# Group normalization on Trainium2: half of each tile's sum moved from the matmuls to two accumulating passes on VectorE

## The chip, the cores and the metric

The kernel runs on one core of a Trainium2 chip. The metric is the device time in microseconds of one execution, and quoted times are medians of several executions. A difference counts as "faster" or "slower" from 2% on.

A ratio in this document is the mean time of one kernel's fast runs over that of the other kernel's fast runs of the same rounds, so it is not quite the ratio of the medians quoted beside it.

## The reference

The input `x` is 128 x 1024 x 32 x 16 in bf16. The 1024 channels form 32 groups of 32, so a group of one sample has 16,384 elements.

```python
xr = x.reshape(B, G, C // G, H, W)                       # G = 32
mu  = xr.mean(axis=(2, 3, 4), keepdims=True)
var = ((xr - mu) ** 2).mean(axis=(2, 3, 4), keepdims=True)
xn  = (xr - mu) / jnp.sqrt(var + 1e-5)
return xn.reshape(B, C, H, W) * g[None, :, None, None] + b[None, :, None, None]
```

## The kernel before

A tile is 128 partitions (4 samples x 32 groups) of F = 16,384 bf16: one partition holds one group of one sample. There are 32 tiles of 4.19 MB. Each is loaded, normalized in place and stored, so 8.4 MB move per tile. Six tile buffers are in flight.

For each tile, TensorE multiplies 512-column slices by an identity matrix and adds them up in PSUM: slices 0 to 7 (a quarter of the tile) into `pa`, slices 8 to 31 into `pb`. VectorE then sums the 512 columns. The first quarter gives an early estimate of the mean, `q`, so that ScalarE can start on the squares. The rest gives the exact mean.

```python
def M(i):                                     # TensorE
    for name, lo, hi in (("pa", 0, MQ), ("pb", MQ, NMM)):      # 8 and 24 slices
        ps = pspool.tile([P, MMN], F32, name=name)
        for k in range(lo, hi):
            ... nc.tensor.matmul(out=ps[:], lhsT=eye[:],
                    rhs=st["xt"][:, k * MMN : (k + 1) * MMN],
                    start=(k == lo), stop=(k == hi - 1)) ...

def R1(i):                                    # VectorE: exact mean
    st["negmean"] = sum_of(st["pb"], st["q"][:], "negmean")
    ...                                       # two 128x1 corrections: off, seed
```

The main loop interleaves tile i with tile i+1. `Q` squares on ScalarE, `V` gets the scales, `A` normalizes a quarter (8 of 32 VectorE instructions of 512 elements), `S` and `L` are the store and the load, both issued by one queue (SP) in program order.

```python
for i in range(NT):
    Q(i)
    if i + 1 < NT: M(i + 1); R0(i + 1)
    V(i)
    for c in range(NQ):
        A(i, c)
        ...
        if c == NQ // 2 - 1 and i + 1 < NT: R1(i + 1)
    ... S(i, 0, NQ) ...                       # the last two tiles are stored in quarters
    j = i + AHEAD                             # AHEAD = 5
    if UPFRONT <= j < NT: L(j)                # waits until the store of tile i-1 has ended
```

## Time and profile before

| | before |
|---|---|
| time, median (range) | 638.12 us (638.1 to 638.38, 3 runs) |
| span of the profile | 636.1 us |
| DMA | 268.4 MB at a mean of 422 GB/s |
| ScalarE / VectorE / TensorE busy | 79% / 65% / 45% |

The first lines are from the page of the profile: busy time, share and instructions of each engine (DVE is VectorE, ACT ScalarE, PE TensorE); DMA busy tenths and GB/s in 40 equal slices; two queues that carry instructions (packets, MB, share); and the chain of work that ended last, by engine and by line.

```profile
...
PE 288.7 (45%) x1025; PEld 113.2 (18%) x1025; DVE 412.6 (65%) x1371; ACT 499.8 (79%) x298; POOL 0.8 (0%) x6
...
DMA  9999999999999999999999999999999999999993
GB/s 373 443 430 398 429 434 432 441 429 431 431 428 433 433 437 427 434 429 429 433 431 436 433 433 431 431 430 435 433 433 435 430 431 429 437 418 439 428 422 151
...
q8 instruction: 8, 0.13, 0.1%
q14 instruction: 15, 0.12, 0.0%
...
DMA 80%; ACT 11%; issue 2%; DVE 2%; PE 1%; SPq 1%; DVEq 0%; ACTq 0%
DMA out_dram<-xt 72%; ACT ja L228 11%; DMA xt<-in_x_dram 8%; DVE xt L305 1%; PE pa L162 1%; SPq L98 1%; DVE jv L245 0%; ACT rstd L258 0%; DVE rstd L266 0%; DVEq L372 0%; DVE bia L277 0%; DVE scl L271 0%; DVE jd L177 0%; ACTq L228 0%; SPq L3
...
```

DMA is over 90% busy in every slice but the last, at about 430 GB/s in the steady part.

The stage table (length, then busy time and count of each engine, granted clock of TensorE, DMA share, GB/s) shows the same level in the middle of the run:

```profile
...
100.00:200.00 100.00, 47.21 (x168) 18.47 (x166) 71.19 (x239) 85.79 (x51) 0.00 (x0) 0.73 1.01 433
...
400.00:500.00 100.00, 46.52 (x160) 18.07 (x160) 66.11 (x221) 78.31 (x48) 0.00 (x0) 0.71 1.00 432
...
```

The table of waits (who waited for whom: us in total, times, longest) says that the engines wait for the loads:

```profile
...
PE pa L162 <- DMA xt<-in_x_dram: 298.8, 32, 19.2
DVE jd L177 <- PE pa L162: 155.8, 25, 9.8
...
```

The issuing queue's own waits show what held its next DMA: mostly an older store that had to end before its buffer could be loaded again.

```profile
...
SPq L98 <- DMA out_dram<-xt: 474.7, 26, 19.5
SPq L318 <- DVE xt L305: 89.3, 12, 26.7
...
```

The timeline of one steady tile (start, length, instruction, and in brackets the idle time before it) shows VectorE's slack.

```profile
...
510.64 0.69 DVE L177 TENSOR_SCALAR_CACHE_REDUCE jd<-pa 128x512 bf16<-128x512 f32 x1 [5.87 <-PE pa L162]
...
512.60 5.25 DVE L305 TENSOR_SCALAR xt<-xt,scl,bia 128x512 bf16<-128x512 bf16 x16
...
517.78 0.73 DVE L177 TENSOR_SCALAR_CACHE_REDUCE jd<-pb,q 128x512 bf16<-128x512 f32 x1
...
518.88 5.25 DVE L305 TENSOR_SCALAR xt<-xt,scl,bia 128x512 bf16<-128x512 bf16 x16
...
530.98 0.69 DVE L177 TENSOR_SCALAR_CACHE_REDUCE jd<-pa 128x512 bf16<-128x512 f32 x1 [6.85 <-PE pa L162]
...
537.05 0.34 SPq L98 DMA_DIRECT2D xt<-in_x_dram  x1
537.43 0.50 SPq L318 DMA_DIRECT2D out_dram<-xt  x1
...
```

Tile 27's first sum starts at 510.64 and tile 28's at 530.98, after 6.85 us of waiting. Between them stands the normalization of tile 26 (2 x 5.25 us), which ends near 524, but its store is issued only at 537.43, right after the load that waited for an older store. So VectorE has 5.5 to 6.9 us to spare in each steady tile, and this finished tile waits 13 us for the queue.

### The profile page before, as it was taken

The page shows a single profiled execution, that of the slowest core. Times are in us where ns is not written, and L with a number is a line of the kernel's source. Part 1 is how long each engine was busy: PE and PEld are TensorE (multiplying, and loading weights), DVE is VectorE, ACT ScalarE, POOL GpSimd, SP SyncE. Part 2 cuts the span into 40 slices and gives each one's busy share as a digit, 9 for nine tenths or more (in the row PEclk, how much of TensorE's full clock was granted, in tenths as well). Part 3 has the DMA queues.
Part 4 walks back from the last instruction along what each step waited for, and adds up shares of the span by engine and source line. Part 5 has one row for each costly group of instructions (what it writes and reads, how often), then busy time and mean ns, then how long its engine had stood idle before and what let it go on. Part 6 is the DMA issues. An engine that isn't in the chain of part 4 may idle for free.

```text
span 636.1 us, 3995 instructions
## 1 busy us (share of the span) xinstructions
PE 288.7 (45%) x1025; PEld 113.2 (18%) x1025; DVE 412.6 (65%) x1371; ACT 499.8 (79%) x298; POOL 0.8 (0%) x6
## 2 busy tenths in 40 slices
PE   5567604563335642356433555425553445546000
PEld 2223201221112210122111222112221112212000
DVE  1388888886686665875567756677555785668740
ACT  4899999997886777977679767797767986779920
POOL 0000000000000000000000000000000000000000
PEclk9789758766788666887567875678765787668655
DMA  9999999999999999999999999999999999999993
GB/s 373 443 430 398 429 434 432 441 429 431 431 428 433 433 437 427 434 429 429 433 431 436 433 433 431 431 430 435 433 433 435 430 431 429 437 418 439 428 422 151
DMA packets 11063, 268.70 MB, mean 422 GB/s; under 512 B 1312, under 2 KB 1312, under 8 KB 1312
## 3 DMA queue, kind: packets, MB, share of 16 engines
q1 hardware_dynamic: 10944, 268.44, 98.3%
q8 instruction: 8, 0.13, 0.1%
q14 instruction: 15, 0.12, 0.0%
q10 hardware_dynamic: 96, 0.00, 0.0%
HBM read 134.22 MB, written 134.22 MB: 422 GB/s over the span
## 4 chain that ended last, share of the span: by engine, by line
DMA 80%; ACT 11%; issue 2%; DVE 2%; PE 1%; SPq 1%; DVEq 0%; ACTq 0%
DMA out_dram<-xt 72%; ACT ja L228 11%; DMA xt<-in_x_dram 8%; DVE xt L305 1%; PE pa L162 1%; SPq L98 1%; DVE jv L245 0%; ACT rstd L258 0%; DVE rstd L266 0%; DVEq L372 0%; DVE bia L277 0%; DVE scl L271 0%; DVE jd L177 0%; ACTq L228 0%; SPq L318 0%
## 5 line engine op out<-in xcount | busy, mean ns | idle before, releaser
L228 ACT ACTIVATE ja<-xt,q 128x4096 bf16<-128x4096 bf16 x128 | 474.2, 3704 | 9.9 <-DVE jd L177 6.8
L305 DVE TENSOR_SCALAR xt<-xt,scl,bia 128x512 bf16<-128x512 bf16 x1016 | 333.5, 405 | 1.2
L162 PE MATMUL pa<-xt,eye 128*128 128x512 bf16 x256 | 109.8, 607 | 298.8 <-DMA xt<-in_x_dram 298.8
L162 PEld LDWEIGHTS <-eye 128*128 128x128 bf16 x1024 | 113.1, 113 | 474.4 <-DMA xt<-in_x_dram 300.2
L162 PE MATMUL pb<-xt,eye 128*128 128x512 bf16 x768 | 184.9, 400 | 1.0 <-DMA xt<-in_x_dram 1.0
L177 DVE TENSOR_SCALAR_CACHE_REDUCE jd<-pa 128x512 bf16<-128x512 f32 x32 | 22.1, 689 | 155.8 <-PE pa L162 155.8
L258 ACT ACTIVATE rstd<-var,eps_t 128x1 f32<-128x1 f32 x32 | 9.4, 294 | 96.4 <-DVE jv L245 96.4
L228 ACT ACTIVATION_READ_ACCUMULATOR ja<-xt,q 128x1 f32 x128 | 23.9, 186 | 0.0
L177 DVE TENSOR_SCALAR_CACHE_REDUCE jd<-pb,q 128x512 bf16<-128x512 f32 x32 | 23.7, 741 | 0.0
L245 DVE TENSOR_SCALAR_CACHE_REDUCE jv<-sq,seed 128x4 f32<-128x4 f32 x32 | 6.8, 214 | 18.9 <-ACT ja L228 18.9
L266 DVE RECIPROCAL rstd<-rstd 128x1 f32<-128x1 f32 x32 | 5.2, 164 | 11.6 <-ACT rstd L258 11.6
L277 DVE SCALAR_TENSOR_TENSOR bia<-scl,negmean,gb 128x32 f32<-128x32 f32 x32 | 8.0, 251 | 1.1
L271 DVE TENSOR_SCALAR scl<-gb,rstd 128x32 f32<-128x32 f32 x32 | 7.7, 242 | 1.1
L198 DVE TENSOR_SCALAR off<-negmean,q 128x1 f32<-128x1 f32 x32 | 6.8, 214 | 1.1
L298 ACT ACTIVATE xt<-xt,bia,scl 128x512 bf16<-128x512 bf16 x8 | 5.8, 800 | 0.8 <-DVE bia L277 0.8
L210 DVE SCALAR_TENSOR_TENSOR seed<-off 128x1 f32<-128x1 f32 x32 | 5.1, 159 | 1.1
L153 DVE COPY gb<-gb_p 128x64 f32<-128x64 f32 x1 | 0.2, 225 | 5.3 <-PE gb_p L145 5.3
L245 DVE DVE_READ_ACCUMULATOR jv<-sq,seed 128x1 f32 x32 | 2.6, 83 | 0.0
L177 DVE DVE_READ_ACCUMULATOR jd<-pa 128x1 f32 x32 | 2.6, 82 | 0.0
L113 ACT ACT_TABLE_LOAD x1 | 1.3, 1283 | 1.7 <-PEq L361 1.7
L177 DVE DVE_READ_ACCUMULATOR jd<-pb,q 128x1 f32 x32 | 2.5, 80 | 0.0
L111 DVE MEMSET eps_t<- 128x1 f32 x1 | 0.1, 59 | 0.9 <-PEq L361 0.9
(10 smaller groups left out, 1.7 us busy)
## 6 DMA issues: line engine op xcount, KB each, us to landing
xt<-in_x_dram SPq DMA_DIRECT2D x30, 4096.0 KB, 29.7
out_dram<-xt SPq DMA_DIRECT2D x30, 4096.0 KB, 39.1
xt<-in_x_dram SPq DMA_DIRECT2D x8, 1024.0 KB, 16.8
out_dram<-xt SPq DMA_DIRECT2D x8, 1024.0 KB, 25.3
gb_b<-in_g_dram ACTq DMA_DIRECT2D x1, 2.0 KB, 3.3
gb_b<-in_b_dram ACTq DMA_DIRECT2D x1, 2.0 KB, 5.3
```

What stands on the lines that cost most here:

```text
L98: nc.sync.dma_start(out=xt[:, c * w : (c + 1) * w], in_=x_v[i][:, c * w : (c + 1) * w]),
L162: nc.tensor.matmul(out=ps[:], lhsT=eye[:], rhs=st["xt"][:, k * MMN : (k + 1) * MMN], start=(k == lo), stop=(k == hi - 1),),
L177: nc.vector.tensor_scalar(out=jd[:], in0=ps[:], scalar1=-inv_n, scalar2=seed, op0=ALU.mult, op1=ALU.add, accum_out=total[:],),
L198: nc.vector.tensor_scalar(out=off[:], in0=st["negmean"][:], scalar1=1.0 / NQ, scalar2=st["q"][:], op0=ALU.mult, op1=ALU.subtract,),
L228: nc.scalar.activation(out=ja[:], in_=st["xt"][:, k * QF : (k + 1) * QF], func=ACT.Square, bias=st["q"][:], scale=1.0 / NQ, accum_out=sq[: ...
L245: nc.vector.tensor_scalar(out=jv[:], in0=st["sq"][:], scalar1=inv_n, scalar2=st["seed"][:], op0=ALU.mult, op1=ALU.add, accum_out=var[:],),
L258: nc.scalar.activation(out=rstd[:], in_=var[:], func=ACT.Sqrt, bias=eps_t[:], scale=float(NQ * NQ),),
L266: chain("dve", nc.vector.reciprocal(out=rstd[:], in_=rstd[:]))
L271: nc.vector.tensor_scalar(out=scl[:], in0=gam, scalar1=rstd[:], scalar2=None, op0=ALU.mult),
L277: nc.vector.scalar_tensor_tensor(out=bia[:], in0=scl[:], scalar=st["negmean"][:], in1=bet, op0=ALU.mult, op1=ALU.add,),
L298: nc.scalar.activation(out=span, in_=span, func=ACT.Identity, bias=bia, scale=scl),
L305: nc.vector.tensor_scalar(out=span, in0=span, scalar1=scl, scalar2=bia, op0=ALU.mult, op1=ALU.add,),
```

## The change

The intent is to relieve TensorE. The matmuls add only slices 0 to 15. The other half of the tile is added on VectorE in two `scalar_tensor_tensor` passes, each of which reads 2048 elements of quarter 2 and 2048 of quarter 3, adds them pairwise and accumulates. A small instruction combines the parts.

```diff
-        for name, lo, hi in (("pa", 0, MQ), ("pb", MQ, NMM)):
+        for name, lo, hi in (("pa", 0, MQ), ("pb", MQ, 2 * MQ)):
 ...
     def R1(i):
         st = state[i]
-        st["negmean"] = sum_of(st["pb"], st["q"][:], "negmean")
+        part = spool.tile([P, 4], F32, name="part")
+        js = jpool.tile([P, HF], BF16, name="js")          # HF = 2048
+        for h in range(2):
+            lo = 2 * QF + h * HF
+            chain("dve", nc.vector.scalar_tensor_tensor(
+                    out=js[:],
+                    in0=st["xt"][:, lo : lo + HF], scalar=1.0,
+                    in1=st["xt"][:, lo + QF : lo + QF + HF],
+                    op0=ALU.mult, op1=ALU.add,
+                    accum_out=part[:, h : h + 1]))
+        half = sum_of(st["pb"], st["q"][:], "half")
+        negmean = spool.tile([P, 1], F32, name="negmean")
+        chain("dve", nc.vector.tensor_scalar(
+                out=part[:, 2:4], in0=part[:, 0:2],
+                scalar1=-inv_n, scalar2=half[:],
+                op0=ALU.mult, op1=ALU.add, accum_out=negmean[:]))
+        st["negmean"] = negmean
```

(Line breaks tightened; the scratch tile of the sums is renamed and widened as well.)

More of the change, by code (lines that the diff above doesn't have):

```diff
@@ L56 @@
     QF = F // NQ
+    HF = QF // 2
     KQ = KC // NQ
@@ L173, in sum_of @@
         total = spool.tile([P, 1], F32, name=name)
-        jd = jpool.tile([P, MMN], BF16, name="jd")
+        jd = jpool.tile([P, HF], BF16, name="js")
         chain(
@@ L177, in sum_of @@
             nc.vector.tensor_scalar(
-                out=jd[:],
+                out=jd[:, 0:MMN],
                 in0=ps[:],
@@ L193, in R1 @@
         st = state[i]
-        st["negmean"] = sum_of(st["pb"], st["q"][:], "negmean")
+        part = spool.tile([P, 4], F32, name="part")
+        js = jpool.tile([P, HF], BF16, name="js")
+        for h in range(2):
+            lo = 2 * QF + h * HF
+            chain(
+                "dve",
+                nc.vector.scalar_tensor_tensor(
+                    out=js[:],
+                    in0=st["xt"][:, lo : lo + HF],
+                    scalar=1.0,
+                    in1=st["xt"][:, lo + QF : lo + QF + HF],
+                    op0=ALU.mult,
+                    op1=ALU.add,
+                    accum_out=part[:, h : h + 1],
+                ),
+            )
+        half = sum_of(st["pb"], st["q"][:], "half")
+        negmean = spool.tile([P, 1], F32, name="negmean")
+        chain(
+            "dve",
+            nc.vector.tensor_scalar(
+                out=part[:, 2:4],
+                in0=part[:, 0:2],
+                scalar1=-inv_n,
+                scalar2=half[:],
+                op0=ALU.mult,
+                op1=ALU.add,
+                accum_out=negmean[:],
+            ),
+        )
+        st["negmean"] = negmean
         off = spool.tile([P, 1], F32, name="off")
```

## The prediction

> **What bounds the kernel now.** DMA. The stage table shows a DMA share of 0.99 to 1.02 at 429 to 433 GB/s from 25 to 600 us (one dip to 412); 268.4 MB at 430 GB/s is 624 of the 636 us. 72% of the chain of waits is stores, in links of about 39 us for two tiles: 19.6 us per tile. The engines wait for it: in the table of waits PE sits 299 us before a tile's first matmul for the load, VectorE 156 us for those matmuls. In the timeline VectorE idles 5.5 to 6.9 us per steady tile.
>
> **What the change does per tile.** Removed: 16 of 32 matmuls, 3.5 us of PE at the dense pitch of 0.22 us. The first 8, which gate the mean estimate, stay. This buys nothing.
>
> Added on VectorE: two scalar_tensor_tensor passes of 2048 bf16 with an accumulator, and a small combining op (0.28 us). The Trainium skill, "Vector Engine (DVE) Microarchitecture Reference", section 5.1, lists the 2x modes for copy, cast, tensor_scalar and tensor_tensor, not for this op, so I assume one column per cycle at the 0.96 GHz of "VectorE: DVE Perf Modes": 2.13 us. The trace agrees with that rate for its accumulating op: 128x512 from PSUM took 0.69 us = 0.53 + 0.16. Estimate: 2.25 us (2.2 to 2.35) per pass, 4.8 us per tile in all, 153 us over 32 tiles. VectorE goes from 413 to about 565 us (89%).
>
> **How much is on the critical path.** Almost none, but it only just fits. A VectorE loop without waits takes 13.5 us now (timeline, tile 3 to tile 4: 15.8 less 2.3 waiting); it becomes 18.3 us, under the 19.6 us of DMA. The passes sit between the halves of the previous tile's normalization, so its store is ready 4.8 us later. In the steady part a finished tile now waits about 13 us (524 to 537 us) until the DMA issuer, held by an older store, sends it; that shrinks to about 8. At the start, stepping the loop with these durations, store 0 goes from 39.9 to 44.6, store 1 from 55.8 to 63, store 2 from 75 to 81 us; queued loads and stores keep DMA busy to 94. VectorE catches up by 1.3 us per tile, so from about tile 9 it waits for loads again. At the end the last tile is normalized by about 615 us instead of 610.7, while earlier stores keep DMA busy to about 615: it just fits.
>
> **Prediction.** 638.4 us, 636.5 to 642 eight times in ten. Faster by over 2%: 1%. Within 2%: 92%. Slower by over 2%: 7%.
>
> **What would show each step.** Matmuls 1025 to 513. Passes of 2.2 to 2.35 us (at 2x near 1.2 us, time unchanged). VectorE busy 550 to 580 us, its wait for PE down from 156 to under 60 us. ScalarE's busy time unchanged. DMA flat at about 430 GB/s with no hole before 110 us. The chain still stores; finished tiles issued on the release of an older store, not of VectorE.
>
> **What would make it wrong.** A pass above about 2.6 us: the loop (13.8 us plus two passes) then nears the DMA period, and soon VectorE bounds everything; at half rate, 4.3 us each, the loop is 22.4 us and the time about 740 us. Or a hole in DMA near 75 to 95 us, or a late last store, costing a few us.

## The result, and the profile after

| | before | after |
|---|---|---|
| time, median (range), same chip | 638.11 us (638.02 to 638.38, 4 runs) | 639.46 us (639.09 to 639.89, 4 runs) |
| ratio | | 1.0021, 95% interval 1.0003 to 1.0038 |
| VectorE busy, instructions | 412.6 us, 1371 | 565.2 us, 1563 |
| matmuls | 1025 | 513 |

The verdict is "same": 1.35 us, or 0.2%, slower. VectorE took on 153 us of work. The page's lines:

```profile
...
PE 187.2 (29%) x513; PEld 65.0 (10%) x513; DVE 565.2 (89%) x1563; ACT 499.8 (78%) x298; POOL 0.8 (0%) x6
...
DMA  9999999999999999999999999999999999999992
GB/s 378 440 430 395 433 434 436 432 430 427 434 436 436 432 425 427 432 440 434 427 430 432 430 438 433 426 427 432 438 440 427 428 432 432 441 413 449 416 425 103
...
q14 instruction: 17, 0.14, 0.1%
q8 instruction: 4, 0.07, 0.0%
...
DVE 52%; DMA 40%; issue 2%; PE 1%; ACT 1%; SPq 1%; DVEq 0%
DMA out_dram<-xt 32%; DVE xt L337 31%; DVE js L202 13%; DMA xt<-in_x_dram 8%; DVE js L178 4%; PE pa L163 1%; ACT rstd L290 1%; DVE bia L309 1%; DVE scl L303 1%; DVE part L216 1%; DVE off L230 1%; DVE rstd L298 1%; SPq L99 1%; DVE jv L277 0%
...
```

DMA is as full as before. The chain of work that ended last now names VectorE for 52% and stores for only 32%. A reader could conclude that VectorE has become the bound for half of the run. The experiments test that.

The group of the new passes (line, engine, operation, shapes, count, busy us and mean ns of one):

```profile
...
L202 DVE SCALAR_TENSOR_TENSOR js<-xt 128x2048 bf16<-128x2048 bf16 x64 | 146.9, 2295 | 2.0 <-DMA xt<-in_x_dram 0.9
...
```

A pass takes 2.29 us. At the 0.96 GHz that the Trainium skill states ("VectorE: DVE Perf Modes", Specifications), 2048 columns at one per cycle are an estimated 2.13 us; 0.16 us is left over. This trace therefore agrees with one column per cycle.

The steady stage still moves 433 or 434 GB/s:

```profile
...
100.00:200.00 100.00, 29.32 (x82) 10.05 (x80) 95.89 (x270) 83.88 (x49) 0.00 (x0) 0.62 1.01 434
...
400.00:500.00 100.00, 28.88 (x80) 10.04 (x80) 91.35 (x253) 79.38 (x46) 0.00 (x0) 0.64 1.01 433
...
```

Of the waits, TensorE's for the loads has grown (373.1 us, 298.8 before), and VectorE's wait for TensorE has shrunk from 155.8 to 24.5 us.

```profile
...
PE pa L163 <- DMA xt<-in_x_dram: 373.1, 30, 15.2
...
DVE js L178 <- PE pa L163: 24.5, 10, 8.1
...
```

In the issuing queue, stores now wait for VectorE's normalization 23 times (204.8 us) and not 12 times (89.3 us):

```profile
...
SPq L99 <- DMA out_dram<-xt: 365.1, 26, 19.4
SPq L350 <- DVE xt L337: 204.8, 23, 31.9
...
```

In a late tile of VectorE's timeline the two passes stand between the halves of the normalization, and 0.68 us of slack is left before the next tile's first sum at 532.06.

```profile
...
512.86 0.69 DVE L178 TENSOR_SCALAR_CACHE_REDUCE js<-pa 128x512 bf16<-128x512 f32 x1 [1.57 <-PE pa L163]
...
514.82 5.26 DVE L337 TENSOR_SCALAR xt<-xt,scl,bia 128x512 bf16<-128x512 bf16 x16
519.99 2.30 DVE L202 SCALAR_TENSOR_TENSOR js<-xt 128x2048 bf16<-128x2048 bf16 x1
...
522.33 2.29 DVE L202 SCALAR_TENSOR_TENSOR js<-xt 128x2048 bf16<-128x2048 bf16 x1
...
526.13 5.25 DVE L337 TENSOR_SCALAR xt<-xt,scl,bia 128x512 bf16<-128x512 bf16 x16
532.06 0.69 DVE L178 TENSOR_SCALAR_CACHE_REDUCE js<-pa 128x512 bf16<-128x512 f32 x1 [0.68 <-PE pa L163]
...
```

### The profile page after: what moved, and what is told of

It is laid out like the page before. It is cut to its first block, busy times and chain, and to the rows that moved or that the text cites. A ratio compares the mean times of both kernels' runs of the same rounds, so it can differ in the third digit from the quotient of the medians.

```text
span 637.8 us, 3191 instructions
## 1 busy us (share of the span) xinstructions
PE 187.2 (29%) x513; PEld 65.0 (10%) x513; DVE 565.2 (89%) x1563; ACT 499.8 (78%) x298; POOL 0.8 (0%) x6
## 4 chain that ended last, share of the span: by engine, by line
DVE 52%; DMA 40%; issue 2%; PE 1%; ACT 1%; SPq 1%; DVEq 0%
DMA out_dram<-xt 32%; DVE xt L337 31%; DVE js L202 13%; DMA xt<-in_x_dram 8%; DVE js L178 4%; PE pa L163 1%; ACT rstd L290 1%; DVE bia L309 1%; DVE scl L303 1%; DVE part L216 1%; DVE off L230 1%; DVE rstd L298 1%; SPq L99 1%; DVE jv L277 0%; DVE seed L242 0%
## 5 line engine op out<-in xcount | busy, mean ns | idle before, releaser
L163 PE MATMUL pa<-xt,eye 128*128 128x512 bf16 x256 | 113.2, 622 | 389.2 <-DMA xt<-in_x_dram 373.1
L202 DVE SCALAR_TENSOR_TENSOR js<-xt 128x2048 bf16<-128x2048 bf16 x64 | 146.9, 2295 | 2.0 <-DMA xt<-in_x_dram 0.9
L163 PEld LDWEIGHTS <-eye 128*128 128x128 bf16 x512 | 64.9, 132 | 519.9 <-DMA xt<-in_x_dram 388.1
L163 PE MATMUL pb<-xt,eye 128*128 128x512 bf16 x256 | 79.7, 467 | 9.5 <-DVE js L178 9.5
L178 DVE TENSOR_SCALAR_CACHE_REDUCE js<-pa 128x512 bf16<-128x512 f32 x32 | 22.3, 697 | 24.6 <-PE pa L163 24.5
L178 DVE TENSOR_SCALAR_CACHE_REDUCE js<-pb,q 128x512 bf16<-128x512 f32 x32 | 24.0, 750 | 4.1 <-DVE js L202 0.5
L216 DVE TENSOR_SCALAR_CACHE_REDUCE part<-part,half 128x2 f32<-128x2 f32 x32 | 6.9, 215 | 1.1
L202 DVE DVE_READ_ACCUMULATOR js<-xt 128x1 f32 x64 | 5.7, 89 | 0.0
L178 DVE DVE_READ_ACCUMULATOR js<-pa 128x1 f32 x32 | 3.0, 94 | 0.0
L216 DVE DVE_READ_ACCUMULATOR part<-part,half 128x1 f32 x32 | 2.7, 83 | 0.0
```

The lines of the kernel that those rows point to most:

```text
L163: nc.tensor.matmul(out=ps[:], lhsT=eye[:], rhs=st["xt"][:, k * MMN : (k + 1) * MMN], start=(k == lo), stop=(k == hi - 1),),
L178: nc.vector.tensor_scalar(out=jd[:, 0:MMN], in0=ps[:], scalar1=-inv_n, scalar2=seed, op0=ALU.mult, op1=ALU.add, accum_out=total[:],),
L202: nc.vector.scalar_tensor_tensor(out=js[:], in0=st["xt"][:, lo : lo + HF], scalar=1.0, in1=st["xt"][:, lo + QF : lo + QF + HF], op0=ALU.mu ...
L216: nc.vector.tensor_scalar(out=part[:, 2:4], in0=part[:, 0:2], scalar1=-inv_n, scalar2=half[:], op0=ALU.mult, op1=ALU.add, accum_out=negmea ...
```

## The experiments

All runs below were each compared with runs of the kernel before on its own chip. Two theories of the extra 1.35 us were put against each other. Theory T: VectorE's added time delays the last tiles and so the last store. Theory F: VectorE's longer instruction stream has to be fetched by DMA, and in a DMA-bound kernel every fetch delays the engine that carries it.

Theory F came from the packet records of the trace. On one DMA engine, a packet starts 3 to 4 ns before the record of the last one ends, and each transfer gives every engine 8 data packets and one of 4 bytes. With these two readings the packets can be assigned to 16 engines (33 to 105 of some 11,000 packets could not be placed in the traces used below, so this is a reconstruction, not a record). Times are counted from the start of the span; the last packet ends 1.3 us before the span does. It gave:

```
trace      span     median engine ends   last engine ends   difference   fetches on the last engine
before     636.1    625.3                634.8               9.5 us      11
after      637.8    623.9                636.5              12.6 us      13
```

So half of the engines are done some 10 us before the last one. The end itself can be read without a reconstruction: at 622 us 16 packets are in flight in both traces, but from 628.4 us (before) and 629.4 us (after) on they come one at a time until the last one. The last engine is the one that carried most of the 8 KB instruction packets. A second reconstruction gave the same ends and counts (11 and 13). In it the last engine stood idle for less than 0.05 us of the whole run, so the moment at which the last store was issued (615.7 us before, 617.4 us after) did not set its end, which speaks against theory T. The 16 KB packets of the other instruction queue fell to other engines, so halving them (8 to 4) took nothing off the last one. A fetch takes about 0.31 us there, and the data packet behind it usually takes 0.35 to 0.65 us longer than its normal 1.21 us.

### e1_matmuls_only: the removal alone

```diff
 # the changed kernel, without the passes; the mean comes from half a tile (wrong on purpose)
-        ... two passes, half, combining op ...
+        st["negmean"] = sum_of(st["pb"], st["q"][:], "negmean")
```

> The removal alone: 16 matmuls a tile fewer, no passes; the mean is then taken from half of the tile, which is wrong on purpose. If PE is no part of the bound, this is the kernel before: 637.8 to 638.4 us, ratio 0.999 to 1.001, with VectorE back at about 412 us busy and its wait for PE at 150 us or more. If the removal was worth something that the passes ate up, it is faster than before by 1 us or more.

Measured: 638.58 us against 637.98 us before, ratio 1.0015 (1.0003 to 1.0028). Taking 512 matmuls away bought nothing, and this kernel was even 0.6 us slower, with every run above the range expected. No theory had that. Runs e11 and e12 below come back to it.

### e2_passes_only: the addition alone

```diff
 # the kernel before: all 32 matmuls stay, the result of the passes is not used
     def R1(i):
         st = state[i]
+        ... part, js, the two passes as in the change ...
         st["negmean"] = sum_of(st["pb"], st["q"][:], "negmean")
+        ... the combining op, into a tile that nobody reads ...
```

> The addition alone: all 32 matmuls kept, the two passes and the combining op added with results that nobody reads. If the whole of the change's 1.35 us comes from what was added on VectorE, this takes as long as the changed kernel: 639.1 to 639.9 us, VectorE busy 565 us. If the removed matmuls helped or hurt, it differs from that by 0.5 us or more.

Measured: 638.84 us, ratio 1.0014 (1.0000 to 1.0027).

```profile
...
PE 286.8 (45%) x1005; PEld 113.0 (18%) x1025; DVE 562.3 (88%) x1563; ACT 499.9 (78%) x298; POOL 0.8 (0%) x6
...
q14 instruction: 17, 0.14, 0.1%
...
```

(The trace lost some records: 1025 matmuls ran, as the 1025 weight loads show.) The median is 0.3 us below the range expected. The addition costs 0.9 us on this chip with no matmul removed. The changed kernel's 639.46 us is 0.6 us more, which by the expectation's own rule leaves room for a cost of the removal.

### e3_tiny_ops: many instructions, little time

```diff
     def R1(i):
         st = state[i]
+        tiny = jpool.tile([P, 1], F32, name="tiny")
+        for _ in range(24):
+            chain("dve", nc.vector.memset(tiny[:], 0.0))
         st["negmean"] = sum_of(st["pb"], st["q"][:], "negmean")
```

> The kernel before plus 24 memsets of 128x1 a tile on VectorE (768 instructions, about 0.06 us each, so 1.5 to 2.4 us a tile, inside the idle 6 us). Theory F: what the change costs is the fetching of VectorE's longer instruction stream, 8 KB packets that all fall to one DMA engine, which ends last; two more of them went with 1.35 us, so six more should cost about 4 to 6 us: 642 to 645 us. Theory T: what it costs is VectorE's added time in the last tiles, which delays the last store; then half of the change's time costs at most 0.7 us: 638 to 638.8 us.

Measured: 642.77 us, ratio 1.0079 (1.0066 to 1.0093): 4.8 us slower, as theory F had it. The memsets are this group:

```profile
...
L196 DVE MEMSET tiny<- 128x1 f32 x768 | 45.3, 59 | 46.6
...
```

They add 45 us of busy time, less than a third of what the change adds, and cost over three times as much. The page of this run shows the instructions and the packets of the queue that follows VectorE's stream:

```profile
...
PE 285.8 (45%) x1005; PEld 112.8 (18%) x1025; DVE 456.6 (71%) x2139; ACT 499.8 (78%) x298; POOL 0.8 (0%) x6
...
q14 instruction: 21, 0.17, 0.1%
...
```

The packets went from 15 to 21. The page "Perfetto Trace Analysis" of the Trainium skill (section "The 4-stage abstract model") states instructions of 64 bytes. By that figure 768 of them are an estimated 48 KB, or six packets of 8 KB, and six more are what the queue shows. The same estimate gives 10.7, 12.2 and 16.7 packets for VectorE's 1371, 1563 and 2139 instructions (before, after, e3), close to the 11, 13 and 17 that the reconstructions put on the last engine. 4.8 us over six packets is 0.8 us each. The reconstruction agrees: the median engine ended at 625.2 us and the last one, with at least 17 fetches, 14.5 us later.

### e4_one_long_op: much time, few instructions

```diff
     def R1(i):
         st = state[i]
+        dead = spool.tile([P, 1], F32, name="dead")
+        chain("dve", nc.vector.tensor_reduce(out=dead[:],
+                in_=st["xt"][:, 2 * QF : 2 * QF + 4480],
+                op=ALU.add, axis=mybir.AxisListType.X))
         st["negmean"] = sum_of(st["pb"], st["q"][:], "negmean")
```

> The kernel before plus a single tensor_reduce of 4480 elements a tile, whose result nobody reads: VectorE's time per tile grows by about 4.8 us as in the change, but by 32 instructions only and not 192. Theory F: 638.1 to 638.6 us. Theory T: 639.2 to 639.7 us, as the changed kernel.

Measured: 637.64 us, ratio 0.9997 (0.9984 to 1.0009), 0.5 us below theory F's range and 1.6 us below theory T's. The page:

```profile
...
PE 287.5 (45%) x1005; PEld 113.2 (18%) x1025; DVE 562.3 (88%) x1403; ACT 499.8 (79%) x298; POOL 0.8 (0%) x6
...
q14 instruction: 15, 0.12, 0.0%
...
```

VectorE is as busy as in e2 (562.3 us in both), the queue of fetches is back at 15 packets, and the cost is gone. This pair is clean evidence for theory F: e2 and e4 ran on the same chip, have the same busy time on VectorE and differ by 160 instructions, two packets and 1.2 us, and their runs don't overlap (638.54 to 639.12 and 637.4 to 638.07). Theory T fell here: in e4 the last tile is normalized at 614.9 us, 4 us later than in the kernel before (610.7), at no cost. One rival was not run: the two also differ in the kind of instruction (e2's passes read two streams and write 2048 elements, e4's reduction writes one), and e2's last tile is done at 616.7 us.

### e5_dose_small and e6_dose_large: where the slack ends

```diff
 # the changed kernel, n = 640 (e5) or 2048 (e6)
+        more = spool.tile([P, 1], F32, name="more")
+        chain("dve", nc.vector.scalar_tensor_tensor(
+                out=js[:, 0:n], in0=st["xt"][:, 0:n], scalar=1.0,
+                in1=st["xt"][:, QF : QF + n],
+                op0=ALU.mult, op1=ALU.add, accum_out=more[:]))
         half = sum_of(st["pb"], st["q"][:], "half")
```

> The changed kernel plus a third, unused pass of 640 elements a tile. VectorE's loop goes from 18.4 to about 19.2 us, still under the 19.6 us that DMA takes per tile. If DMA is the bound throughout, the time moves only by what 64 more instructions cost in fetches (half a packet): 639.3 to 640.3 us. If VectorE already bounds the changed kernel, as 52% of its chain of waits says, 0.8 us times 31 tiles is added: about 664 us.

Measured for e5: 642.29 us, ratio 1.0069 (1.0054 to 1.0085). Both numbers missed: it is 2 us above the first range and 22 us below the second. In the page DMA stays full until slice 36 and then has a hole (391, 194, 367 GB/s):

```profile
...
PE 186.9 (29%) x503; PEld 65.1 (10%) x513; DVE 591.0 (92%) x1627; ACT 499.8 (78%) x298; POOL 0.8 (0%) x6
...
GB/s 383 436 424 401 437 434 426 432 432 436 430 428 430 440 431 426 438 430 436 426 430 436 435 432 425 434 438 432 427 434 438 434 426 430 439 426 391 194 367 353
...
```

The timeline shows VectorE's loop and its end:

```profile
...
548.25 0.21 DVE L290 TENSOR_SCALAR_CACHE_REDUCE jv<-sq,seed 128x4 f32<-128x4 f32 x1
...
567.55 0.21 DVE L290 TENSOR_SCALAR_CACHE_REDUCE jv<-sq,seed 128x4 f32<-128x4 f32 x1
...
626.14 7.84 DVE L350 TENSOR_SCALAR xt<-xt,scl,bia 128x512 bf16<-128x512 bf16 x24
```

The loop is 567.55 - 548.25 = 19.30 us, still under the 19.6 us of DMA. But VectorE starts late and gains only 0.3 us per tile, so it does not catch up with the loads before the end. The last tile is normalized at 626.14 + 7.84 = 634.0 us, and the last stores have no other transfers left to hide behind. The expectation had counted the loop and not the lag. Up to slice 36 the rates are those of the kernel before, so DMA was the bound up to there.

> The changed kernel plus a third, unused pass of 2048 elements a tile. VectorE's loop becomes about 20.7 us, over the 19.6 us of DMA: now VectorE bounds the kernel. The last tile's normalization ends near 677 us and the time is about 683 us (676 to 692). If instead the passes are hidden whatever their length, it stays under 645 us.

Measured for e6: 687.75 us, ratio 1.0782 (1.0767 to 1.0796), inside the range. The loop is now longer than DMA's and VectorE does bound the kernel; DMA falls to about 400 GB/s in the middle of the run. So the passes are hidden only because they fit.

### e7_copy_only: the floor of DMA

```diff
-    M(0); R0(0); GB(); R1(0)
     for i in range(NT):
-        ... Q, M, R0, V, A, R1 ...
         ... S(i) and L(i + AHEAD) as before ...      # wrong on purpose: a copy
```

> Loads and stores alone in the same order and sizes; nothing is computed, the result is wrong on purpose. VectorE has a handful of instructions and no stream to fetch. Theory F (the engine that carries the fetches of VectorE's stream ends about 10 us after the other 15): all engines end together and the time is 626 to 630 us. If DMA bandwidth alone sets the time, it is 636 to 638 us, as before.

Measured: 632.98 us (631.89 to 634.27), ratio 0.9924 (0.9909 to 0.9938). The result is wrong by design. It falls between the two expectations.

```profile
...
GB/s 368 433 431 424 435 433 431 433 431 433 424 433 433 433 428 433 433 433 433 435 431 433 435 433 433 426 437 435 433 431 428 433 433 433 433 424 437 433 420 277
...
q14 instruction: 1, 0.01, 0.0%
...
```

With one instruction packet left, 5 us go away. The reconstruction puts the median engine at 624.1 us, as in the other traces, and the last one 4.8 us later (in the fastest of four runs, which spread over 2.4 us). This run took away all computing with the fetches, so it does not isolate them. By e3's 0.8 us per fetch, an estimate, they could explain the larger part of the last engine's delay, but not all of it. The rest, in which some data packets took longer with no fetch beside them, stays unexplained.

### e8_pool_share, e9_pool_share_8, e10_pool_share_12: fewer instructions on VectorE

If instructions on VectorE cost time, fewer should save some. Part of the normalization goes to GpSimd.

```diff
 # the kernel before, in A(i, c)
+                pool = i < NT - 1 and k % KQ >= KQ - POOL_SHARE   # 1, 2, 3 in e8, e9, e10
                 chain(
-                    "dve", nc.vector.tensor_scalar(
+                    "pool" if pool else "dve",
+                    (nc.gpsimd if pool else nc.vector).tensor_scalar(
```

> The kernel before, with 8 of the 32 normalization instructions of a tile on GpSimd: 248 instructions fewer on VectorE, so about two fetches fewer. Theory F: 1.5 to 2 us faster than before, 636 to 636.8 us, if GpSimd's own stream is fetched by another DMA engine and GpSimd keeps up (8 instructions in under 12 us a tile). Theory of a bound by bandwidth alone: 638 us. If GpSimd takes over 2 us each, it becomes the bound and this is slower.

e8 had a share of 1, so 4 of 32 instructions and 124 fewer on VectorE, not the 8 and 248 of the text. Measured: 637.97 us against 637.93, ratio 1.0003 (0.9991 to 1.0016). By the figure of e3, 124 instructions are an estimated one packet fewer for VectorE, but with GpSimd's own stream the queue shows 16 in all, one more than before. So this tells nothing apart.

> What e8 was described as: 8 of the 32 normalization instructions of a tile on GpSimd, 248 fewer on VectorE (e8 as run had only 4 of 32, 124 fewer, and GpSimd took 0.83 us each). About two fetches of VectorE's stream fewer at the 0.8 us each of e3: 636.3 to 636.9 us against 638. If other engines' streams or chance set the end by now, 637.5 to 638.5 us.

Measured for e9: 637.76 us against 638.30 before, ratio 0.9992 (0.9978 to 1.0005). It lies in the range of the rival, and the interval includes no change: inconclusive.

> 12 of 32 on GpSimd, 372 fewer on VectorE: about three fetches fewer, 635.5 to 636.2 us by theory F; GpSimd then works about 10 us a tile, under the 19.6 us of DMA. If fetches below the number of the kernel before are worth nothing, 637.5 to 638.5 us; if GpSimd and VectorE hold each other up for more than VectorE's idle 6 us a tile, slower.

Measured for e10: 636.97 us, ratio 0.9979 (0.9966 to 0.9992). The interval excludes no change, so this kernel beats both by their ratios, and the kernel before by 1.3 us on the same chip. It is less than expected, and the only one of three such tries whose gain is clear of the noise, so it supports theory F and does not prove it. Its groups show what else it did:

```profile
...
L307 DVE TENSOR_SCALAR xt<-xt,scl,bia 128x512 bf16<-128x512 bf16 x644 | 347.7, 611 | 1.2
L307 POOL TENSOR_SCALAR xt<-xt,scl,bia 128x512 bf16<-128x512 bf16 x372 | 297.2, 814 | 297.6 <-PE pb L163 197.6 <-DVE bia L278 100.0
...
```

GpSimd takes 0.81 us per instruction, and VectorE's own instruction went from 405 to 611 ns. The Trainium skill ("SBUF — State Buffer", section "SBUF: two separate sides") states that a VectorE instruction in a two-port mode and a GpSimd instruction block each other on a shared port pair. This trace agrees in that VectorE's instructions became longer beside GpSimd's; the lock itself is not visible. VectorE had slack for it, and no cost shows in the time. Moving the work also adds GpSimd's own stream (18 packets in all on the queue, 15 before), so the saving on the last engine seems to be partly a shift to other engines: in the reconstruction the last engine carries 9 fetches and ends 8.3 us after the median engine.

### e11_removal_long_op and e12_half_width: was e1 real?

```diff
 # e11: e1 plus the tensor_reduce of e4
 # e12: the kernel before, but the 24 matmuls of pb read 256 columns each (wrong mean on purpose)
+            wd = MMN if name == "pa" else MMN // 2
-                        rhs=st["xt"][:, k * MMN : (k + 1) * MMN],
+                        rhs=st["xt"][:, k * MMN : k * MMN + wd],
```

> e1 and e4 together: 16 matmuls a tile gone (mean from half a tile, wrong on purpose) and one tensor_reduce of 4.8 us, so the changed kernel's time on VectorE and PE with 128 fewer VectorE instructions (1435 for 1563). If the removal itself costs the 0.6 us that e1 showed, 638.4 to 638.9 us; if e1 was chance, 637.6 to 638.2 us. As the changed kernel, 639.2 us or more, only if time and not instructions counts.

Measured for e11: 638.43 us against 638.30, ratio 0.9999 (0.9987 to 1.0012). The time alone lies in the range expected if the removal costs 0.6 us. But the kernel before was 0.3 us slower on this chip than on that of e1, so the ratio is the fair reading: no cost of the removal is seen, and none of 4.8 us more VectorE time per tile (562.0 us busy) with it. This repeats e4 with the removal in place. (The text put e11 at 1435 instructions; the profile counts 1403, as in e4.)

> The kernel before with its 24 second-group matmuls of a tile at half width, 256 columns (a wrong mean on purpose): as many PE instructions, about 40% less PE work. If e1's 0.6 us came from a shorter PE instruction stream, this is the kernel before, 637.6 to 638.2 us; if from less PE work, 638.4 to 638.9 us.

Measured for e12: 638.43 us, ratio 1.0001 (0.9989 to 1.0014). Again the time lies in the range expected if less TensorE work costs time, but the ratio shows no such cost. The 0.6 us of e1 was not found again in e11, which has the same removal. What made e1 slower stays open; it is a tenth of a per cent, as much as the intervals of e11 and e12 leave room for.

## Why the prediction was right

The time (638.4 predicted, 639.46 measured, inside 636.5 to 642) held. Point by point:

- **DMA bounds the kernel: right.** The rate stayed at 430 to 434 GB/s. Taking TensorE work away (e1, e11, e12) and adding 4.8 us of VectorE work per tile in one instruction (e4) changed nothing beyond 0.15%. More instructions to fetch (e3), and more VectorE time than the slack and the lag allow (e5, e6), did.
- **The removed matmuls buy nothing: right,** by e1, e11 and e12.
- **The size of the addition: right.** 2.29 us per pass for an estimate of 2.25, VectorE at 565.2 us for "about 565", its loop at 18.42 us for 18.3.
- **"From about tile 9 it waits for loads again": wrong.** VectorE first waits for TensorE again (more than 0.1 us) at 433.6 us, for tile 23. The catch-up rate was right (1.2 us per tile for 1.3 predicted). The lag was mis-sized: in the trace before, the load of tile 6 and its first 8 matmuls are done at 97.5 us, while VectorE on the new loop reaches that tile only at about 118.5 us. 21 us at 1.2 us per tile is 18 tiles.
- **"The chain still stores; finished tiles issued on the release of an older store, not of VectorE": wrong for the first 340 us,** for the same reason. While VectorE lags behind the loads, each store goes out the moment VectorE is done, so the chain names VectorE for 52%. It did not cost anything, because stores and loads already queued kept DMA full; e4 has nearly the same lag (it first waits again at 353.5 us) and no cost. A chain says what released what, not whether another resource was full meanwhile.
- **"A pass above about 2.6 us": right as a place, too lax as a reason.** e5 has the loop that passes of about 2.7 us would give, 19.3 us, and lost 4 us although the loop is below DMA's period. The limit that e5 points to is that VectorE must have caught up before the last tile; where exactly it lies was not run. The last normalization ended at 617 us in the changed kernel (615 predicted), when the last DMA engine still had work for 19 us, and at 634 us in e5.
- **Not foreseen: the 1.35 us itself.** It lay inside the predicted range, but for no reason named there. That the time came within 1.1 us of 638.4 is therefore partly luck. It fits two more fetches at the 0.8 us of e3; e3 shows that more instructions cost, e4 that time on VectorE does not. The exact split of the 1.35 us is not settled: e2 gives 0.9 us for the addition, and the rest is of the size of e1's unexplained 0.6 us.

## What to carry to other kernels

When DMA is full, an engine's idle time per tile is a budget: work that fits is free, but count the lag from the start of the run too, because an engine that starts late must catch up before the last tile. Don't read a chain of waits as the bound without looking at whether DMA had a hole. And in a kernel bound by DMA, try few long instructions in place of many short ones: here VectorE's instruction stream travelled on the same DMA engines as the data, at about 0.8 us for each 8 KB.

## What the Trainium skill lacked or had wrong

- "Runtime: NRT & Kernel Launch", section "Instruction fetch mechanics", says that the stream is refilled in 16 KiB blocks and that crossing a block is "mostly hidden". The queue that follows VectorE's stream moved packets of 8 KB (768 more instructions, six more packets), and each cost about 0.8 us of kernel time (e3: 4.8 us for six), while DMA was full and, in the reconstruction, one DMA engine carried most of them. The other instruction queue, whose count fell from 8 to 4 as the matmuls halved, did move 16 KB packets.
- "Trainium Architecture — The Big Picture", section "The software stack", has the streams moved at load time. Here packets of them travel throughout the run (15 on one queue before, 21 in e3), as the page of the first point has it.
- "Vector Engine (DVE) Microarchitecture Reference", section 5.1, does not name `scalar_tensor_tensor`. With an accumulator, on two bf16 sources in SBUF, it ran at one column per cycle: 2.29 us for 2048. Whether it would be faster without the accumulator was not run.
- "SBUF — State Buffer", in its table of bandwidths, gives HBM to one core as about 358 GB/s. Reads and writes together ran at 430 to 434 GB/s here with one core active, near the 436 GB/s that the same table gives for DMA to SBUF. Other pages of the skill do say that the lower figure is a share that a core running alone exceeds; this table doesn't.
- No page says how late the DMA engine that carries most of the instruction fetches ends when DMA is full: the median engine was done 9.5 us before the last one in the kernel before, and 4.8 us even with almost no instructions to fetch (e7).
